# Decode block with its backward pass: V loads queued one iteration later, and seven V tiles of batch 0 kept instead of six

## The chip, the cores and the metric

The kernel runs on one core of a Trainium2 chip. The metric is the device time of one launch in microseconds (us). Five runs of the kernel before gave 923.03 to 930.29 us, with a median of 924.86 us.

## The reference

The computation is one decode step of a transformer block (two sequences, one token each) and its gradients.

```python
h = x + A(layernorm(x))            # attention against a cache, 32 heads, 4096 keys of 128
h2 = h + B(layernorm(h))           # dense layer 640 -> 1728 -> 640 with relu
# A: q = x @ wq; s = q k^T * Dh**-0.5; p = softmax(s); o = p v; o @ wo
out, vjp = jax.vjp(f, A_x, A_k_cache, A_v_cache, A_wq, A_wo, B_w1, B_w2)
grads = vjp(grad_out)              # out, and a gradient for each of the seven inputs
```

For each of the 64 pairs of batch and head, K (4096 x 128, bf16, 1 MB) and V (the same size) are read. Their gradients gK and gV, of the same size again, are written. Everything else is small next to these 256 MB. The gradient of the scores needs V once more: dp = go V^T, where go is the gradient of the head's output, which is known only when the forward pass of the whole batch row and the dense layer are done.

## The kernel before, in words

The work is written out by hand in one order. A plan is a list of pairs (i, j). With i, a step of phase 1 (`p1_iter`) is emitted: scores, softmax and weighted sums of head i. With j, a step of phase 2 (`p2_iter`): the gradients gK and gV of turn j. Steps 0 to 31 are phase 1 of batch 0. Steps 32 to 40 are phase 1 of batch 1 alone, while the dense layer of batch 0 and the go of its first heads are worked out in small background pieces in between. From step 41 every second step has a turn of phase 2 too (the mixed stage, to step 65). After that phase 2 runs alone, with the outer products of the weight gradients beside it.

`p1_iter(i)` is a pipeline over three heads. It transposes K(i) on TensorE in four groups (L416), copies them out of PSUM (L421), and multiplies them by q (L427). It does the softmax of head i-1 and multiplies K(i-1) by it on VectorE (L478). And for head i-2 it multiplies V(i-2) with this product (L471, 32 matmuls, first used right after the first two transpose groups of K(i) and a small matmul L517). K(i-1)'s buffer is given back in the sixth of eight parts of iteration i, V(i-2)'s in the last.

`p2_iter(j)` transposes V again (L437), multiplies it by go (L450), and makes gV and gK by outer products on VectorE (L823), which GpSimd's queue stores.

K, V, the second reading of V (called W) and some weight pieces are loaded by the SP queue, strictly in the order of one list, `queue`. It is built before the work is emitted. For plan step n it gets: perhaps a piece of wq, then K(i), then the W that step n+1 will need, then V(i-1), then perhaps other weights. `pump`, called after each part, takes loads from the head of the list as long as a buffer is free. There are twelve buffers of 1 MB for all these. So the list sets the order, and the giving back of a buffer sets when the next load can be issued.

`KEPT` says of how many last heads of each batch V stays in its buffer from phase 1 to phase 2; for these no W is loaded. `turns` puts them first in phase 2. So before, the buffers that are left for the other loads fall from twelve to six towards the middle. When the first three kept tiles have been used, their buffers become output buffers for gK and gV; nine stay for loads.

`middle_gen` takes the heads of a batch for go in groups: first two kept heads, then the other kept heads, then groups of up to eight. A go takes one reduction on VectorE (L650) per head, and `bg_until` sees to it that a turn's go is there before its turn.

Of the kernel before, what the change touches and what calls it, by code (L numbers as in the profile page):

```python
# [15 lines left out]
def kernel(  # L16
# [101 lines left out]
    def share(**want):  # L118

        wanted.clear()  # L120
        wanted.update(want)
        for tag in homes:
            while free[tag] > 0 and goes_to(tag) != tag:
                to = goes_to(tag)
                homes[to].append(homes[tag].pop(0))
                for d in (free, owned):
                    d[tag] -= 1
                    d[to] += 1

    def more_home(tag, pool):  # L130
        homes[tag].append(len(pools))
        pools.append(pool)
        free[tag] += 1
        owned[tag] += 1
# [256 lines left out]

    pairs = [(b, h) for b in range(B) for h in range(H)]
    NP1 = len(pairs)
    KEPT = (6, 5)
    turns = [(b, h) for b in range(B) for h in (*range(H - KEPT[b], H), *range(H - KEPT[b]))]
    turn_of = {bh: j for j, bh in enumerate(turns)}
    kept = {(b, h) for b in range(B) for h in range(H - KEPT[b], H)}
    u_bank = [None]
# [325 lines left out]
    def middle_gen(b):  # L724
# [66 lines left out]

        first = H - KEPT[b]
        bounds = [(first, first + 2), (first + 2, H)] if b == 0 else [(first, H)]
# [271 lines left out]
    while i <= NP1 + 1 or j <= NP1:  # L1065
        ii = i if i <= NP1 + 1 else None
# [7 lines left out]
    queue = []  # L1074
    W_AT = (10, 15, 20, 24, 31)
    W2_AT = (8, 13, 18)
    for n, (ii, jj) in enumerate(plan):
        if ii is not None:
            if ii % QP == 3 and (ii + 3) // QP < NQ:
                queue.append(("wq", (ii + 3) // QP))  # L1080
            if ii < NP1:
                queue.append(("K", ii))
        ahead = plan[n + 1][1] if n + 1 < len(plan) and ii is not None else jj
        if ahead is not None and ahead < NP1 and turns[ahead] not in kept and ("W", ahead) not in queue:
            queue.append(("W", ahead))
        if ii is not None and 1 <= ii <= NP1:
            queue.append(("V", ii - 1))
        if ii in W_AT:
            queue.append(("w", W_AT.index(ii)))
        if ii in W2_AT:  # L1090
            queue.append(("w2", W2_AT.index(ii)))
# [34 lines left out]
    for n, (i, j) in enumerate(plan):  # L1126
# [4 lines left out]
        if i is None and plan[n - 1][0] is not None:  # L1131
            pkp.release()
            big1 = tc.alloc_tile_pool(name="big1", bufs=1)
            more_home("ld", big1)
            share(ld=KEPT[1] + 4, g=4)
        if all_go and not late[0]:
# [6 lines left out]
        if fin is not None and not bg2 and not bg3:  # L1143
            share(ld=8 + 3 * more, g=6 + 3 * more)
        elif fin is not None and j >= H + KEPT[1] - 1:
            share(ld=5 + 2 * more, g=4 + 2 * more, f=3 + more, q=2 + more)
# [99 lines left out]
```

## Time and profile before

| | before |
|---|---|
| median of 5 runs | 924.86 us |
| the profiled execution | 925.49 us |
| its span | 923.6 us |
| PE, DVE, ACT, POOL busy | 760.3, 662.4, 531.0, 168.4 us |
| moved by DMA | 363.04 MB, mean 393 GB/s |
| Kt, Vt, Wt loads of 1 MB | 64, 64, 53 |
| gK, gV stores of 1 MB | 64, 64 |
| mean granted TensorE clock | 0.784 |

Times in the profile are us from the span's start. The DMA share is the mean busy share of the sixteen DMA engines. A load's landing time is counted from its issue on the SP queue, so it holds the wait behind other transfers too. An engine's idle time costs nothing where another engine or the transfers set the pace.

### The profile page before, as it was taken

The numbers are of one execution on the slowest core, as the hardware profiler recorded it, in microseconds if no ns is written. First come the engines' busy times: TensorE is split into PE (matmuls) and PEld (weight loads), VectorE is DVE, ScalarE is ACT, GpSimd is POOL, SyncE is SP. The second block draws the span as 40 slices with busy tenths as digits, with TensorE's granted clock in tenths as the row PEclk, the third lists the DMA queues.
The fourth block names the chain that finished last, engine by engine and source line by source line (L and its number), as shares of the span: only waits on it lengthen the run. The fifth ranks groups of instructions, "written<-read, shape, count | busy, mean of one in ns | idle before, by whom it ended". The sixth has DMA issues, their size and how long they took to land.

```text
span 923.6 us, 26951 instructions
## 1 busy us (share of the span) xinstructions
PE 760.3 (82%) x11482; PEld 639.8 (69%) x11482; DVE 662.4 (72%) x1237; ACT 531.0 (57%) x1082; POOL 168.4 (18%) x329
## 2 busy tenths in 40 slices
PE   5998998999988898798878826966878887888892
PEld 5887787888877787687767726755757566666661
DVE  4654786876777888678778879868698454558774
ACT  4564564556776777577733625544646555557661
POOL 1222222223200101011011112111122111112211
PEclk9998999999999999899995866556655557556556
DMA  8999999998789999999999999999999999989998
GB/s 345 418 399 411 404 395 411 410 415 321 291 318 363 365 399 422 423 392 422 423 388 396 406 426 379 399 379 408 398 402 388 426 424 425 423 358 355 423 422 352
DMA packets 59480, 363.04 MB, mean 393 GB/s; under 512 B 5696, under 2 KB 15552, under 8 KB 19168
## 3 DMA queue, kind: packets, MB, share of 16 engines
q1 hardware_dynamic: 37920, 212.18, 58.2%
q0 software_dynamic: 18432, 134.23, 35.0%
q10 hardware_dynamic: 3008, 14.91, 4.1%
q8 instruction: 90, 1.47, 0.6%
q14 instruction: 30, 0.25, 0.1%
HBM read 212.16 MB, written 149.13 MB: 391 GB/s over the span
## 4 chain that ended last, share of the span: by engine, by line
PE 39%; DMA 29%; DVE 15%; ACT 10%; issue 5%; POOL 0%; ACTq 0%; POOLq 0%; SPq 0%; DVEq 0%
DMA Kt<-in_A_k_cache_dram 13%; DMA out_dram<-gK 9%; PE t_ps L437 8%; PE t_ps L416 7%; PE m_ps L471 7%; DMA out_dram<-gV 5%; DVE gV L823 4%; DVE gK L823 4%; ACT t_sb L421 4%; PE o_ps L927 3%; DMA wqs<-in_A_wq_dram 3%; PE s_ps L427 3%; ACT t_sb L442 2%; DVE pk L478 2%; PE u_ps L500 2%
## 5 line engine op out<-in xcount | busy, mean ns | idle before, releaser
L421 ACT COPY t_sb<-t_ps 128x1024 bf16<-128x1024 bf16 x223 | 217.4, 1017 | 60.6 <-PE t_ps L416 59.9
L442 ACT COPY t_sb<-t_ps 128x512 f32<-128x512 f32 x256 | 149.4, 587 | 147.4 <-PE t_ps L437 143.8
L437 PE MATMUL t_ps<-ident_f,Wt 128*128 128x128 f32 x848 | 193.5, 375 | 3.2 <-ACT t_sb L421 2.8
L478 DVE TENSOR_TENSOR pk<-Kt,ep 128x2048 bf16<-128x2048 bf16 x128 | 156.4, 1222 | 54.1 <-ACT ep L526 26.2
L416 PE MATMUL t_ps<-ident_bf,Kt 128*128 128x128 bf16 x2048 | 155.2, 226 | 27.3 <-DMA Kt<-in_A_k_cache_dram 21.0
L471 PE MATMUL m_ps<-pk,Vt 128*128 128x129 bf16 x2048 | 172.6, 223 | 1.1 <-ACT OU L584 1.1
L823 DVE TENSOR_TENSOR gK<-rb,gsp 128x2048 bf16<-128x2048 bf16 x128 | 152.3, 1225 | 22.4 <-DMA out_dram<-gK 16.2
L823 DVE TENSOR_TENSOR gV<-rb,pp 128x2048 bf16<-128x2048 bf16 x128 | 152.6, 1218 | 20.9 <-DMA out_dram<-gV 13.9
L437 PEld LDWEIGHTS t_ps<-ident_f,Wt 128*128 128x128 f32 x848 | 134.5, 195 | 27.8 <-issue 18.4
L416 PEld LDWEIGHTS <-Kt 128*128 128x128 bf16 x2048 | 127.3, 101 | 35.0 <-DMA Kt<-in_A_k_cache_dram 22.0
L471 PEld LDWEIGHTS <-Vt 128*128 128x128 bf16 x2048 | 126.7, 99 | 29.4 <-issue 29.4
L450 PEld LDWEIGHTS <-t_sb 128*128 128x128 bf16 x2048 | 95.6, 106 | 39.3 <-ACT t_sb L442 19.1
L450 PE MATMUL dp_ps<-gom,t_sb 128*128 128x2 bf16 x2048 | 95.2, 168 | 9.4 <-ACT t_sb L442 8.3
L488 POOL COPY pk<-ep 128x16 bf16<-128x16 bf16 x80 | 64.0, 803 | 194.9 <-ACT ep L526 165.7
L427 PE MATMUL s_ps<-qc,t_sb 128*128 128x1 bf16 x2048 | 88.1, 164 | 3.7 <-ACT t_sb L421 2.5
L861 POOL DMA_DIRECT2D out_dram<-gK x64 | 34.0, 531 | 282.8 <-DVE gK L823 212.7
L880 POOL DMA_DIRECT2D out_dram<-gV x64 | 34.2, 534 | 265.1 <-DVE gV L823 220.0
L427 PEld LDWEIGHTS <-t_sb 128*128 128x128 bf16 x2048 | 77.2, 96 | 6.7 <-ACT t_sb L421 3.4
L936 ACT CAST ot<-o_ps 128x512 bf16<-128x512 f32 (+4 forms) x134 | 59.4, 479 | 13.9 <-DMA out_dram<-ot 7.8
L583 ACT CAST MT<-m_ps 128x128 bf16<-128x128 f32 x64 | 17.1, 266 | 74.9 <-PE m_ps L471 74.8
L650 DVE CUSTOM_DVE_ANT_0 junk<-wo_t,hbc 128x640 bf16<-128x640 bf16 x64 | 52.4, 818 | 0.2
L850 ACT ACTIVATE rb<-dp_ps,rt 128x256 bf16<-128x256 f32 x64 | 30.4, 475 | 36.1 <-PE dp_ps L845 35.4
(195 smaller groups left out, 785.0 us busy)
## 6 DMA issues: line engine op xcount, KB each, us to landing
Kt<-in_A_k_cache_dram SPq DMA_DIRECT2D x64, 1024.0 KB, 14.0
Vt<-in_A_v_cache_dram SPq DMA_DIRECT2D x64, 1024.0 KB, 14.7
out_dram<-gV POOLq DMA_DIRECT2D x64, 1024.0 KB, 11.4
out_dram<-gK POOLq DMA_DIRECT2D x64, 1024.0 KB, 10.5
Wt<-in_A_v_cache_dram SPq DMA_DIRECT2D x53, 1024.0 KB, 12.8
wo_t<-in_A_wo_dram SPq DMA_DIRECT2D x4, 1280.0 KB, 19.3
wqs<-in_A_wq_dram SPq DMA_DIRECT2D x5, 1024.0 KB, 18.8
wq_t<-in_A_wq_dram SPq DMA_DIRECT2D x5, 960.0 KB
```

Of the source, the lines that this page charges most:

```text
L416: nc.tensor.transpose(t_ps[:, j, :], nat[:, g * GT + j, :], ident_bf[:])
L421: nc.scalar.copy(out=t_sb[:], in_=t_ps[:])
L427: nc.tensor.matmul(dst[:, sc:sc + 1], lhsT=t_sb[:, j, :], rhs=vec, start=True, stop=True)
L437: nc.tensor.transpose(t_ps[:, j, :], natf[:, 2 * cc:2 * cc + 2, :].rearrange("p c k -> p (c k)"), ident_f[:])
L442: nc.scalar.copy(out=t_sb[:], in_=t_ps[:])
L450: nc.tensor.matmul(dst[:, sc:sc + 2], lhsT=v[:, j, :, par], rhs=vecs[:, par, :], start=(par == 0), stop=(par == 1))
L471: nc.tensor.matmul(r["m"][:, 0:129], lhsT=r["V"][:, sc, :], rhs=r["pk"][sc // HALF][:, sc % HALF, 0:129], start=(sc == 0), stop=(sc == NSC ...
L478: nc.vector.tensor_tensor(out=p["pk"][k][:, :, 0:128].rearrange("p s (a two) -> p s a two", two=2), in0=p["K"][:, sl, :].rearrange("p s (a ...
L488: nc.gpsimd.tensor_copy(out=col, in_=e)
L650: nc.vector.tensor_tensor_reduce(out=junk[0:kc, 0:width], in0=in0, in1=in1, scale=1.0, scalar=0.0, op0=ALU.mult, op1=ALU.add, accum_out=acc)
L823: nc.vector.tensor_tensor(out=pairs_view(dst[:, sl, :]), in0=row.rearrange("p (a two) -> p a two", two=2)[:, None, :, :].to_broadcast([128 ...
L936: nc.scalar.copy(out=ot[0:P, k, n0:n0 + nn], in_=o_ps[0:P, 0:nn])
```

## The change

Two edits, both in how the loads are listed. V(i-2), not V(i-1), is put into the list at step i, so each V stands one step later, behind K(i) and behind the W of the next step, and its load is issued in the iteration that comes one later. The list ends with V(63) at step 65. And seven last heads of batch 0, 25 to 31, keep their V; the first seven turns of phase 2 are these heads, and head 0 is turn 7. W is loaded for 52 turns. The middle's groups of go heads become (25, 26), (27 to 31), then 0 to 7, 8 to 15, 16 to 23 and 24.

```diff
-    KEPT = (6, 5)
+    KEPT = (7, 5)
@@ the list of loads, at plan step n with (ii, jj)
         ahead = plan[n + 1][1] if n + 1 < len(plan) and ii is not None else jj
         if ahead is not None and ahead < NP1 and turns[ahead] not in kept and ("W", ahead) not in queue:
             queue.append(("W", ahead))
-        if ii is not None and 1 <= ii <= NP1:
-            queue.append(("V", ii - 1))
+        if ii is not None and ii >= 2:
+            queue.append(("V", ii - 2))
```

## The prediction, made before the result

> **What bounds the kernel now.** I read the page first: how full the sixteen DMA engines are in each of the 40 slices, and how fast they move data.
>
> ```profile
> span 923.6 us, 26951 instructions
> ...
> PE 760.3 (82%) x11482; PEld 639.8 (69%) x11482; DVE 662.4 (72%) x1237; ACT 531.0 (57%) x1082; POOL 168.4 (18%) x329
> ...
> DMA  8999999998789999999999999999999999989998
> GB/s 345 418 399 411 404 395 411 410 415 321 291 318 363 365 399 422 423 392 422 423 388 396 406 426 379 399 379 408 398 402 388 426 424 425 423 358 355 423 422 352
> ```
>
> The DMA engines are full nearly everywhere (363 MB at 393 GB/s), except in slices 10 to 12 and a little after. The busy times by stage (window, then busy us and count of each engine, the granted clock, the DMA share, GB/s) say where exactly:
>
> ```profile
> core 0: us, PE busy (x) PEld busy (x) DVE busy (x) ACT busy (x) POOL busy (x), PEclk, DMA share, GB/s
> 0.00:208.00 208.00, 185.07 (x3585) 162.68 (x3586) 134.72 (x286) 112.75 (x221) 55.81 (x110) 0.97 1.01 401
> 208.00:269.00 61.00, 57.23 (x1131) 50.68 (x1128) 46.08 (x126) 42.02 (x79) 15.86 (x28) 0.97 0.82 313
> 269.00:320.00 51.00, 44.26 (x830) 38.78 (x828) 39.81 (x87) 36.98 (x77) 6.16 (x8) 1.00 0.90 348
> 320.00:466.00 146.00, 126.52 (x2350) 112.72 (x2346) 112.15 (x227) 101.60 (x212) 14.72 (x25) 0.95 1.01 413
> 466.00:923.00 457.00, 347.17 (x3610) 274.98 (x3606) 329.68 (x513) 237.65 (x495) 75.89 (x158) 0.60 0.99 399
> ```
>
> Batch 0's scores (to 208 us), the mixed stage from 320 and the gradients from 466 run at a DMA share of 0.99 to 1.01: transfers set their pace. The middle (208 to 269, iterations 32 to 40, no stores) is different: share 0.82, and PE busy 57.2 of 61.0. Time added there is added to the end, because the transfers can't use it. Now the SP queue's own timeline in the middle (start, duration of the issue, instruction):
>
> ```profile
> 243.27 0.33 SPq L458 DMA_DIRECT2D Kt<-in_A_k_cache_dram  x1
> 243.69 0.38 SPq L458 DMA_DIRECT2D Vt<-in_A_v_cache_dram  x1
> 249.70 0.33 SPq L458 DMA_DIRECT2D Kt<-in_A_k_cache_dram  x1
> 250.12 0.38 SPq L458 DMA_DIRECT2D Vt<-in_A_v_cache_dram  x1
> 255.92 0.33 SPq L458 DMA_DIRECT2D Kt<-in_A_k_cache_dram  x1
> 256.34 0.38 SPq L458 DMA_DIRECT2D Vt<-in_A_v_cache_dram  x1
> ```
>
> One K and one V per iteration, each the moment a buffer comes free, V 0.4 us behind K. The first pair is K38 and V37. V's landing in this stretch (225 to 302 us, the tile view of Vt), and PE's timeline where iterations 38 and 39 begin:
>
> ```profile
> DMA to landing us min/median/max: 6.8/7.6/7.9
> ```
>
> ```profile
> 248.11 1.07 PE L416 MATMUL t_ps<-ident_bf,Kt 128*128 128x128 bf16 x16
> 249.83 0.23 PE L517 MATMUL s_ps<-neg_ident,rmax 128*128 128x128 bf16 x1 [0.66 <-ACT t_sb L421]
> 249.93 0.63 PE L471 MATMUL m_ps<-pk,Vt 128*128 128x129 bf16 x8
> ...
> 256.42 0.63 PE L471 MATMUL m_ps<-pk,Vt 128*128 128x129 bf16 x8
> ```
>
> The reader is to see the distance: K38 is first used at 248.11, V36 at 249.93. V is needed only 1.8 us after K.
>
> **The change part by part.** *One load less.* Head 25's V stays in its buffer, so one of 53 W loads goes: 1.05 MB, at 393 to 415 GB/s 2.5 to 2.7 us of DMA time. What it is worth depends on what is prefetched when the middle ends. Counting the owners of the twelve buffers at the start of iteration i there: before, six kept and K(i), K(i-1), V(i-2), V(i-1), K(i+1), V(i); after, seven kept and K(i), K(i-1), V(i-2), K(i+1), V(i-1). One V less is prefetched, one W less is wanted: what remains to be moved after the middle is the same. The saving is spent as more idle DMA time in the middle, so I cost it at 0 (best case -2.7).
>
> *K one load earlier in the full stretch to 208 us.* An iteration needs K(i), and 1.8 us or less later V(i-2). Before, V(i-2) lay ahead of K(i) in the queue; now it lies behind. The same bytes must land before the first L471, so only the little work between the two uses starts earlier. At iteration 32, where the full stretch ends, K32 is used at 210.0 and V30 at 210.9; K32 would land about 2.6 us earlier, at 207.4, V30 at 210.0 to 210.4. Gain 0.5, at most 2.6.
>
> *V with two buffers in turn, not three.* This is the cost. V(i) now takes the place in the queue, and the buffer release, where before V(i+1) was issued; K's places don't move. PE takes instructions in order, so a late V holds all behind L471: m_part, the next transposes L416, the scores L427, the interleaved gradient matmuls L437 and L450, and so ACT's and DVE's work on them. Issue place of before's next V, plus landing time, less before's first use of V(i):
> - V36: 243.7 + 7.6 = 251.3, used at 249.9: 1.4 late
> - V37: 250.1 + 7.6 = 257.7, used at 256.4: 1.3 late
> - V38: 256.3 + 7.6 = 263.9, used at 263.5: 0.4 late
> - V39: 262.8 + 7.6 = 270.4, used at 269.7: 0.7 late
> - V40 to V44: 0.2 to 2.8 us early.
>
> V(i) is used two iterations on, and its issue moves only with delays up to iteration i, so delay D obeys D(i+2) = max(D(i+1), D(i) + lateness): 1.4, 1.4, 1.8, 2.1. The middle costs 2.1 us.
>
> Here a rule can be set against the row. The Trainium skill ("DMA: Bandwidth & Descriptors", section "Anatomy of one DMA — SWDGE (gpsimd) path") puts a transfer, on GpSimd's path, at 2.0 us plus bytes at 436 GB/s: 4.4 us for one tile, 6.8 with a K just ahead. V36 would be 0.6 late, V37 0.5, V38 and V39 none: 0.6 us. These loads come from SP, and the trace has 5.0 for K and 7.6 for V, so I take the row, 2.1.
>
> With the stores of the mixed stage, landings grow. The V issued at 328.2 took 9.7 us; from 345 on the least is 10.2, the median 15.3. On the same footing: V45, 311.4 + 9.7 against 319.4, 1.7 late; V47, 328.2 + 9.7 against 335.5, 2.4 late; V49, 342.6 + 10.2 against 350.4, 2.4 late; V46 and V48 on time; V50 onward early, because nine load buffers with few kept give the Vs room again (the first W load now comes two iterations later too). Sum 6.5. The skill's section "Queues, rings and completion order" says that a DMA engine takes turns between queues packet by packet. A load beside a store would then have half the rate: 2.0 + 4 x 2.4 = 11.6 us for a V behind a K, where the row has 9.7. By the rule V45 and V47 would be 3.6 and 4.3 late, and the mixed sum 10.3. I take the row again. How much of 6.5 counts? Transfers are full from 320, and PE later waits for K (1.4 at 366.6, 5.7 at 387.3, 3.4 at 439.8), so a delay can run into a wait that exists anyway. But it delays stores and buffer releases too. Bounds 0 and 6.5; nothing in the trace separates them, I take half, 3.2.
>
> *The end of the scores.* W(12) and W(13) now stand ahead of V62 and V63. V63 takes the place of 464.9 instead of 456.8; with about 8 us it lands at 472.9, used at 470.8: 2.1 late, in a full stretch; half, 1.0 (bounds 0 and 2.1).
>
> *Order of the go work.* The second group of batch 0 has five heads, not four, so one reduction of 0.82 us on DVE (L650) moves forward, none is added; it is due at iteration 45. If its slots were gone it would cost at most those 0.8 us. Taken at 0.
>
> Sum: -0.5 + 2.1 + 3.2 + 1.0 = +5.8 us. The profiled execution took 925.5 us (span 923.6 and 1.9 around it), 0.6 above the median of 924.9; on the median 930.7, say 930.5.
>
> **The rivals.** *All of the lateness counts* (and repeats): 2.1 + 6.5 + 2.1 - 0.5 = +10.2, 935; by the take-turns rule +14, 939. For it: PE, in order, stands 1.8 us behind K. Against: transfers are full from 320. *The delay is hidden*: V lands as the page's figure has it, and the mixed stage absorbs the rest: -0.5 + 0.6 to 2, about 925.5. For it: margins in the middle are about 1 us, within what DMA times scatter. *Faster*: PE's waits for K go.
>
> ```profile
> PE t_ps L416 <- DMA Kt<-in_A_k_cache_dram: 21.0, 9, 5.7
> ```
>
> Nine waits, 21.0 us. With K one load (2.5 us) earlier each could lose up to 2.5; taken wait by wait that is 15 us at most. It decides if V isn't what is waited for next, which needs V's use more than 2.5 us behind K's; 1.0 to 1.8 is seen. With half of it, 917.5. Last, *it doesn't do what it says*: W for the next iteration still goes ahead of V for this one, so the order isn't by need in the mixed stage; that is in the sum as V63.
>
> **How the numbers follow.** Chances: the forecast (927 to 936) 0.46, all of it counting (935 to 942) 0.14, hidden (921 to 928.5) 0.26, faster 0.14. The predicted time is the first's, 930.5. Leaving out the top of the second and most of the last gives 919.5 to 939. A measurement of this kernel tells about 0.5%, 4.6 us, from no change: slower means above 929.5. The first case lies above it with 0.37 of its 0.46, the second wholly: 0.51. Same: 0.09 + 0.25 = 0.34. Faster: 0.14 + 0.01 = 0.15.
>
> **What would show it.** After: 52 Wt loads; a wait of L471 for the DMA of Vt, none before, of 1 to 2 us near 250 and 2 us or more between 320 and 355; the waits of L416 for Kt down; a DMA share in 208 to 269 below 0.82. The forecast is wrong if L471 shows no such waits (hidden), or if the stretch from 320 to 466 is shorter than 146 us (faster).

## The result, and the profile after

The changed kernel takes 928.96 us (median of 29 runs), the kernel before 924.89 us (50 runs beside them). The ratio is 1.0045, with a 95% interval of 1.0031 to 1.0058: 4.1 us slower, where 5.6 were forecast (930.5 against 924.9). The lines of the page that answer to those shown of before:

```profile
span 927.9 us, 26947 instructions
...
PE 768.7 (83%) x11482; PEld 644.9 (70%) x11482; DVE 663.5 (72%) x1237; ACT 531.9 (57%) x1082; POOL 174.7 (19%) x329
...
DMA  9999999997779989999999999999999999989998
GB/s 345 417 396 409 407 394 409 412 415 300 288 260 345 348 326 423 423 422 421 423 395 396 409 425 396 405 410 391 401 413 393 426 426 424 420 344 368 421 418 343
```

One load is gone: 361.99 MB instead of 363.04. Yet slices 10 to 15 move less in sum (1,867 instead of 2,057 in the six GB/s figures). The busy times by stage of the changed kernel (columns as before):

```profile
core 0: us, PE busy (x) PEld busy (x) DVE busy (x) ACT busy (x) POOL busy (x), PEclk, DMA share, GB/s
0.00:208.00 208.00, 186.86 (x3594) 163.06 (x3595) 134.96 (x286) 112.79 (x221) 55.73 (x110) 0.97 1.01 400
208.00:269.00 61.00, 56.20 (x1061) 49.68 (x1058) 43.50 (x118) 40.18 (x76) 16.11 (x25) 0.92 0.74 278
269.00:320.00 51.00, 44.71 (x816) 39.03 (x813) 37.80 (x83) 35.72 (x75) 4.97 (x11) 0.97 0.89 337
320.00:466.00 146.00, 126.62 (x2310) 111.98 (x2308) 112.57 (x227) 101.99 (x209) 19.17 (x26) 0.94 0.99 406
466.00:923.00 457.00, 354.35 (x3722) 281.15 (x3718) 334.70 (x527) 241.27 (x504) 78.70 (x159) 0.60 1.00 404
```

In the middle (208 to 269) the DMA share fell from 0.82 to 0.74, and 278 GB/s instead of 313 over 61 us are 2.1 MB less moved, two loads. One is the V that is no longer prefetched; the other I put down to the delay. Two columns moved that the prediction had not looked at. PE is hardly less busy in the middle (56.2 instead of 57.2) although it executed 70 matmuls fewer, and its granted clock fell from 0.97 to 0.92. PE's waits for transfers, from the view of waits:

```profile
PE m_ps L471 <- DMA Vt<-in_A_v_cache_dram: 21.0, 16, 2.9
```

Before, it was nine waits of L416 for Kt, also 21.0 us in sum. The tile that is waited for has changed; the sum has hardly changed (three waits for Kt, 3.4 us, are left beside these). Now the middle itself: the SP queue's timeline, and then PE's, of the changed kernel.

```profile
242.46 0.33 SPq L458 DMA_DIRECT2D Kt<-in_A_k_cache_dram  x1
242.88 0.38 SPq L458 DMA_DIRECT2D Vt<-in_A_v_cache_dram  x1
248.71 0.33 SPq L458 DMA_DIRECT2D Kt<-in_A_k_cache_dram  x1
249.13 0.67 SPq L458 DMA_DIRECT2D Vt<-in_A_v_cache_dram  x1
258.18 0.33 SPq L458 DMA_DIRECT2D Kt<-in_A_k_cache_dram  x1
```

```profile
247.29 1.07 PE L416 MATMUL t_ps<-ident_bf,Kt 128*128 128x128 bf16 x16
248.84 0.23 PE L517 MATMUL s_ps<-neg_ident,rmax 128*128 128x128 bf16 x1 [0.49 <-DVE rmax L573]
251.30 1.05 PE L471 MATMUL m_ps<-pk,Vt 128*128 128x129 bf16 x8 [2.23 <-DMA Vt<-in_A_v_cache_dram]
...
252.55 1.04 PE L416 MATMUL t_ps<-ident_bf,Kt 128*128 128x128 bf16 x8
...
255.23 1.04 PE L500 MATMUL u_ps<-pk,hot 128*32 128x512 bf16 x8
...
258.44 1.05 PE L416 MATMUL t_ps<-ident_bf,Kt 128*128 128x128 bf16 x16
```

The V at 242.88 is V36: the same place in the queue, 0.4 us behind K38, held V37 before. PE finishes the first transposes of K38, and then waits 2.23 us for V36. What follows is not only later but slower: the eight V matmuls take 1.05 us instead of 0.63, L500 1.04 instead of 0.62. From V36's first use to K39's it is 7.1 us (251.3 to 258.4); before, it was 4.8 (249.9 to 254.7). K39's first use before:

```profile
254.70 1.07 PE L416 MATMUL t_ps<-ident_bf,Kt 128*128 128x128 bf16 x16
```

How far iteration i is behind the kernel before, from the first L416 of each (us; one profiled execution of each kernel, all but the first are experiments):

| | K32 | K38 | K39 | K44 | K45 | K47 | K48 | K52 | K56 | K60 | K61 | K63 | span |
|---|---|---|---|---|---|---|---|---|---|---|---|---|---|
| changed | -1.5 | -0.8 | +3.7 | +2.6 | +4.8 | +3.8 | +8.3 | +9.9 | +2.7 | +9.1 | +5.5 | +5.1 | +4.2 |
| seven kept alone | +0.2 | +3.6 | +4.4 | +5.0 | +6.8 | +10.3 | +11.6 | +14.2 | +5.5 | +11.9 | +9.0 | +10.0 | +8.3 |
| V later alone | -2.3 | -1.9 | -2.2 | -2.0 | -2.1 | -2.0 | -2.0 | -2.0 | -4.7 | -1.3 | -4.9 | -1.3 | -4.3 |
| eight kept, V later | -2.2 | +13.0 | +17.3 | +41.3 | +42.5 | +49.6 | +55.3 | +62.0 | +51.9 | +58.9 | +55.3 | +57.2 | +56.7 |
| changed, waits filled | -2.5 | +1.2 | +3.6 | +3.8 | +4.6 | +4.0 | +7.0 | +8.3 | +0.3 | +5.7 | +2.4 | +3.7 | +4.7 |
| one W less | 0.0 | +0.2 | 0.0 | 0.0 | +0.2 | -0.6 | -0.5 | +0.3 | -4.8 | -0.1 | -1.1 | -0.5 | -2.9 |

In the changed kernel there are two steps of 4.5 us: at V36 (K38 to K39), and at V45 (K47 to K48, a wait of 2.49 us at 325.9, again with slow matmuls behind it). Between them stands a third, of 2.2 us (K44 to K45), which is not a wait for a load. It is the go work of the second group, heads 27 to 31. Before, VectorE was through with the reductions of that group, then four heads, at 285.6 us:

```profile
285.58 0.17 DVE L673 CAST goc<-go 128x4 bf16<-128x4 f32 x1
```

In the changed kernel the fifth reduction (L650) comes behind a gV product that waits for an output buffer, and PE waits for the group:

```profile
299.93 1.23 DVE L823 TENSOR_TENSOR gV<-rb,pp 128x2048 bf16<-128x2048 bf16 x1 [3.27 <-DMA out_dram<-gK]
301.07 0.82 DVE L650 CUSTOM_DVE_ANT_0 junk<-wo_t,hbc 128x640 bf16<-128x640 bf16 x1
...
301.94 0.17 DVE L673 CAST goc<-go 128x5 bf16<-128x5 f32 x1
```

```profile
302.16 0.19 PE L337 MATMUL pr_ps<-goc,sel 128*128 128x5 bf16 x2 [2.63 <-DVE goc L673]
```

The kernel before waits in this iteration too, 2.11 us at 300.8 for a copy of ScalarE, but at full clock from there on; in the changed kernel the clock is at half for 3.4 us behind the wait. All four profiles with seven kept have this wait of L337 (2.2 to 2.8 us), those with five, six or eight have none.

In the full stretch behind, 7 us of 9.9 are gone at K56, but they come back: it is 9.1 at K60. Most of that dip belongs to the profile of before, which waited 5.7 us for K55. The run with one W less issues the same loads in the same order as the kernel before until past K63; it is level with it at K52 and K60, and 4.8 us ahead at K56. So one column of this table can be off by about 5 us. What does go is 3.6 us at K61, where the kernel before waited 3.4 us for K61 and the changed one did not.

### The profile page after: what moved, and what is told of

Read it like the earlier page. It is cut to its first block, busy times and chain, and to the rows that moved or that the text cites. A ratio compares the mean times of both kernels' runs of the same rounds, so it can differ in the third digit from the quotient of the medians.

```text
span 927.9 us, 26947 instructions
## 1 busy us (share of the span) xinstructions
PE 768.7 (83%) x11482; PEld 644.9 (70%) x11482; DVE 663.5 (72%) x1237; ACT 531.9 (57%) x1082; POOL 174.7 (19%) x329
## 2 busy tenths in 40 slices
DMA packets 59336, 361.99 MB, mean 390 GB/s; under 512 B 5680, under 2 KB 15536, under 8 KB 19152
## 4 chain that ended last, share of the span: by engine, by line
PE 33%; DMA 32%; DVE 11%; ACT 7%; issue 4%; POOL 0%; SPq 0%; POOLq 0%; ACTq 0%; DVEq 0%
DMA Vt<-in_A_v_cache_dram 15%; PE t_ps L437 8%; DMA out_dram<-gV 7%; DMA out_dram<-gK 7%; PE m_ps L471 6%; PE t_ps L416 5%; DVE gV L823 4%; DVE gK L823 3%; DMA wqs<-in_A_wq_dram 3%; PE o_ps L927 2%; ACT t_sb L442 2%; PE dp_ps L450 2%; ACT t_sb L421 2%; PE u_ps L500 2%; PE s_ps L427 2%
## 5 line engine op out<-in xcount | busy, mean ns | idle before, releaser
L437 PE MATMUL t_ps<-ident_f,Wt 128*128 128x128 f32 x832 | 191.5, 378 | 2.6 <-ACT t_sb L421 2.6
L471 PE MATMUL m_ps<-pk,Vt 128*128 128x129 bf16 x2048 | 175.4, 226 | 21.4 <-DMA Vt<-in_A_v_cache_dram 21.0
L823 DVE TENSOR_TENSOR gV<-rb,pp 128x2048 bf16<-128x2048 bf16 x128 | 152.6, 1218 | 21.7 <-DMA out_dram<-gV 8.5
L471 PEld LDWEIGHTS <-Vt 128*128 128x128 bf16 x2048 | 127.9, 100 | 55.3 <-issue 31.3
L823 DVE TENSOR_TENSOR gK<-rb,gsp 128x2048 bf16<-128x2048 bf16 x128 | 152.4, 1225 | 17.9 <-DMA out_dram<-gK 14.0
L416 PE MATMUL t_ps<-ident_bf,Kt 128*128 128x128 bf16 x2048 | 157.6, 228 | 8.6 <-DMA Kt<-in_A_k_cache_dram 3.4
L416 PEld LDWEIGHTS <-Kt 128*128 128x128 bf16 x2048 | 129.4, 102 | 15.7 <-issue 8.3
L450 PEld LDWEIGHTS <-t_sb 128*128 128x128 bf16 x2048 | 95.9, 106 | 38.0 <-ACT t_sb L442 19.1
L427 PEld LDWEIGHTS <-t_sb 128*128 128x128 bf16 x2048 | 78.9, 98 | 3.5 <-DVE t_sb L419 1.3
L650 DVE CUSTOM_DVE_ANT_0 junk<-wo_t,hbc 128x640 bf16<-128x640 bf16 x64 | 52.3, 818 | 0.2
## 6 DMA issues: line engine op xcount, KB each, us to landing
Wt<-in_A_v_cache_dram SPq DMA_DIRECT2D x52, 1024.0 KB, 11.9
```

Source lines behind the costliest of these rows:

```text
L416: nc.tensor.transpose(t_ps[:, j, :], nat[:, g * GT + j, :], ident_bf[:])
L427: nc.tensor.matmul(dst[:, sc:sc + 1], lhsT=t_sb[:, j, :], rhs=vec, start=True, stop=True)
L437: nc.tensor.transpose(t_ps[:, j, :], natf[:, 2 * cc:2 * cc + 2, :].rearrange("p c k -> p (c k)"), ident_f[:])
L450: nc.tensor.matmul(dst[:, sc:sc + 2], lhsT=v[:, j, :, par], rhs=vecs[:, par, :], start=(par == 0), stop=(par == 1))
L471: nc.tensor.matmul(r["m"][:, 0:129], lhsT=r["V"][:, sc, :], rhs=r["pk"][sc // HALF][:, sc % HALF, 0:129], start=(sc == 0), stop=(sc == NSC ...
L650: nc.vector.tensor_tensor_reduce(out=junk[0:kc, 0:width], in0=in0, in1=in1, scale=1.0, scalar=0.0, op0=ALU.mult, op1=ALU.add, accum_out=acc)
```

## The experiments

Ratios are to runs of the kernel before on the same chip, with 95% intervals.

**The two edits apart.** Theory A: the seventh kept tile takes a buffer from the middle, and whichever tile then has two buffers in turn and not three comes late. Theory B: V's place in the queue makes it late.

```diff
# seven kept alone (from the kernel before)
-    KEPT = (6, 5)
+    KEPT = (7, 5)
# V later alone (from the changed kernel)
-    KEPT = (7, 5)
+    KEPT = (6, 5)
```

> Seven V tiles of batch 0 kept, V listed where the kernel before lists it (V(i-1) at step i). Theory A (rotation: the seventh kept tile takes a buffer from the loads of the middle, and whichever tile loses its third buffer comes late): in the middle five buffers hold K(i), K(i-1), V(i-2), V(i-1), K(i+1), so now K(i+2) takes the later place behind V(i). K38 would land at 243.7 + 7.6 = 251.3 against a use at 248.1: 3 us late, K40 and K41 1 to 2 us; waits of L416 for Kt in the middle, none of L471 for Vt, and a time no better than that of the change: 929 to 935. Theory B (the queue's order alone makes V late): no cost here, and one load less: 922 to 925.

> Six V tiles kept, V listed one step later as in the change. Theory A: the middle has six buffers for K(i), K(i-1), V(i-2), K(i+1), V(i-1), K(i+2); V(i) is issued no later than in the change but a K is far ahead of it, so it lands in about 5 us instead of 7.6: no wait of L471 in 230 to 300 us, the time 923 to 926, equal to before. Theory B (order): V still stands behind K and W, so the waits of L471 stay and the time is 928 to 930.

Seven kept alone: 933.14 us, 1.0104 (1.0079 to 1.0129). V later alone: 923.06 us, 0.9986 (0.9962 to 1.0010). From the views of waits in 208 to 320 us, first seven kept alone, then V later alone:

```profile
PE t_ps L416 <- DMA Kt<-in_A_k_cache_dram: 6.6, 4, 4.0
```

```profile
PE m_ps L471 <- DMA Vt<-in_A_v_cache_dram: 1.4, 1, 1.4
```

Theory A holds, B is out. With seven kept in the old order K is late (K38 by 4.0 us); with V later and six kept PE waits for no load in this window after the one wait at 210. Of the two edits the kept tile costs about 9 us, and V's later place wins about half of that back. The table says the same: seven kept alone has lost 14.2 us at K52. Not all of the 9 us is the buffer: the wait for the go work, 2.2 us in this run, comes with the seventh head as well, and what it is worth in the end was not tested apart.

**One buffer less still.**

```diff
-    KEPT = (7, 5)
+    KEPT = (8, 5)
```

> The change with eight V tiles of batch 0 kept (one W load less again, one buffer less again in the middle). Theory A: four buffers hold K(i), K(i-1), V(i-2), K(i+1); V(i-1) can be issued only when K(i-1) is given back in iteration i and is used about 4 us later, so it comes 1 to 3 us late in every iteration from about 34 to 48, and the time rises by 15 to 40 us, to 945 to 970. Theory B (order): V's place in the list is that of the change, so the time stays within 926 to 932.

980.09 us, 1.0620 (1.0553 to 1.0687): 56 us, above what A said. Waits in 208 to 320 us and the busy times there:

```profile
PE m_ps L471 <- DMA Vt<-in_A_v_cache_dram: 29.1, 9, 4.6
```

```profile
208.00:269.00 61.00, 46.49 (x800) 41.02 (x798) 32.05 (x84) 31.35 (x58) 14.35 (x19) 0.81 0.58 218
269.00:320.00 51.00, 35.67 (x540) 31.10 (x538) 25.07 (x65) 23.56 (x45) 4.64 (x12) 0.79 0.49 187
```

V is late in every iteration, as A said, but by up to 4.6 us where A had 1 to 3. That is one part of why the size was off. The other is the granted clock of 0.8 there: the trace's record of it shows half clock for 3.4 to 6.8 us behind nearly every one of these waits. Of the 38 us that the delay grew from K33 to K43 (320 us), 28 are the waits themselves.

**Is the half clock part of the price?** In the two iterations with the long waits matmuls without use fill the time in which PE would wait.

```diff
+        if i in (38, 47):
+            for k in range(32):
+                nc.tensor.matmul(p["bank"][:, 320:448], lhsT=c["K"][:, k % 16, :], rhs=c["K"][:, k % 16 + 1, :],
+                                 start=True, stop=True)
         if r is not None:
             m_part(0)
             m_part(1)
```

> The changed kernel with 32 matmuls without use (128x128, on K that is there) put ahead of the V matmuls L471 of iterations 38 and 47 alone, where the changed kernel's PE waited 2.2 and 2.5 us for V36 and V45 and ran at half clock for 6.8 us behind each wait. V still lands when it lands. Theory A1 (the half clock is part of the price): the granted clock stays at 1.00 from 251 to 258, K39's first use goes from 3.7 us behind the kernel before to 1 to 2 us behind, and the whole to 926 to 927.5. Theory A2 (the time behind the wait is hidden later by full transfers): K39 comes earlier all the same, but the whole stays at 928 to 930.

929.46 us, 1.0043 (1.0027 to 1.0059). The window of 251 to 258 us, in the kernel before, the changed kernel and the filled one, and the filled one's PE timeline:

```profile
251.00:258.00 7.00, 6.33 (x132) 5.55 (x130) 6.86 (x19) 5.33 (x12) 1.68 (x4) 1.00 0.85 315
```

```profile
251.00:258.00 7.00, 6.70 (x78) 5.41 (x79) 3.87 (x8) 2.65 (x5) 2.36 (x2) 0.51 0.63 265
```

```profile
251.00:258.00 7.00, 6.23 (x114) 5.43 (x115) 5.00 (x14) 3.60 (x7) 2.06 (x3) 1.00 0.82 308
```

```profile
252.00 1.95 PE L522 MATMUL s_ps<-Kt 128*128 128x128 bf16 x32 [0.64 <-DVE nb L519]
253.79 0.63 PE L471 MATMUL m_ps<-pk,Vt 128*128 128x129 bf16 x8
...
256.17 0.62 PE L500 MATMUL u_ps<-pk,hot 128*32 128x512 bf16 x8
```

Locally the clock's part is shown. With PE busy through the wait the clock stays at 1.00, L471 takes 0.63 us, and the steps in the table shrink from 4.5 to 2.4 us (K38 to K39) and from 4.5 to 3.0 (K47 to K48). But the whole did not gain: A2 was right, or the gain is below the 1 to 2 us that these intervals leave open. This profile also has a half-clock stretch of its own, 209.5 to 216.3, behind a wait of 1.4 us for V30, which cost 3.8 us between K32 and K33; the changed kernel's wait there was 0.6 us, without it. So a microsecond won at one place can be lost at another from one execution to the next. The wait for the go work, 2.4 us here, is not touched by the filling.

**V ahead of W.**

```diff
+        if ii is not None and ii >= 2:
+            queue.append(("V", ii - 2))
         ahead = plan[n + 1][1] if n + 1 < len(plan) and ii is not None else jj
         if ahead is not None and ahead < NP1 and turns[ahead] not in kept and ("W", ahead) not in queue:
             queue.append(("W", ahead))
-        if ii is not None and ii >= 2:
-            queue.append(("V", ii - 2))
```

> The change with one exchange: at each step V(i-2) is listed ahead of the W of the next step (order of need throughout). If the W ahead of V costs in the mixed stage: the wait of 2.1 us of L471 at 478 goes and those at 393 to 463 shrink, time 1 to 2 us below the change, about 927. If the mixed stage and its end are set by transfers anyway, the waits move to W or K and the time stays at 928 to 930. The waits at 251 and 326 stay under both, because no W is loaded before 350.

> Six kept, V one step later, and V ahead of W. Six kept with V later showed no V wait in the middle and 0.9986 of before; its waits of L471 from 360 to 470 come with a W ahead of V. If those cost: 1 to 2 us less than with W first, 921 to 922. If transfers set that stretch: 922.5 to 924, as with W first.

With seven kept 929.55 us, 1.0065 (1.0040 to 1.0090); with six kept 924.59 us, 0.9986 (0.9959 to 1.0014), the same ratio as with W first. With seven kept the wait for V63 at 478 is gone, the waits at 250 and 324 are there (2.4 us each), and five waits of 0.5 to 2.3 us remain in 390 to 462. In the full stretch V's place beside W is worth nothing that these intervals can show.

**What a load is worth.** One W load left out where transfers are full, and one W load added by keeping five, with V later and with V as before.

```diff
# one W less (from the kernel before), in p2_iter and in the list
+        if j == 19:
+            S2[20] = {"W": c["W"]}
+        else:
             give(c["W"], "g" if j < H and owned["g"] < 3 else None)
-        if ... turns[ahead] not in kept and ("W", ahead) not in queue:
+        if ... turns[ahead] not in kept and ahead != 20 and ("W", ahead) not in queue:
# five kept
+    KEPT = (5, 5)
```

> The kernel before, but turn 20 takes the W tile of turn 19 (its dp and gK are then of the wrong head): one load of 1.05 MB left out, all buffers and the order of V as before, and no effect on the middle. If a load in the full stretch is worth its transfer time: 2.5 to 2.7 us faster than before, about 922. If the stretch is set by something else: equal to before, 924 to 925.

> Five kept, V one step later: one buffer more in the middle than with six, one W load more. By the count of buffers the extra load is fetched in the idle transfer time of the middle and costs nothing: 922 to 925, the same as with six kept and V later (923.1). If a load costs its transfer time wherever it is: 2.6 us more, 925.5 to 926.5.

> Five kept, V listed as before. By the count of buffers the middle has a seventh one for one more prefetched tile, and the one more W load is paid there: equal to before, 924 to 926. If a load costs its transfer time anywhere: 2.6 us more, about 927.5.

One W less: 923.16 us, 0.9972 (0.9956 to 0.9989): 2.6 us (1.0 to 4.1), which agrees with the transfer time. Five kept: with V later 923.58 us, 0.9977 (0.9959 to 0.9996), with V as before 925.33 us, 0.9999 (0.9977 to 1.0021). So a load costs about 2.6 us in the full stretch, but the load that a sixth kept tile saves costs nothing when it is put back: an added 2.6 us (1.0028) lies outside both intervals. The freed buffer prefetches more in the middle, as the row of five kept with V as before shows (share 0.86 and 333 GB/s, against 0.82 and 313 in the kernel before):

```profile
208.00:269.00 61.00, 56.03 (x1135) 49.45 (x1131) 46.49 (x128) 42.44 (x80) 15.58 (x28) 1.00 0.86 333
```

A kept tile's saving is paid with the buffer that it sits in.

**Six kept in batch 1.** V's later place gives a buffer back at the end of the scores. Can one more tile of batch 1 be kept for it?

```diff
-    KEPT = (7, 5)
+    KEPT = (6, 6)          # and (5, 6)
-            share(ld=KEPT[1] + 4, g=4)
+            share(ld=KEPT[1] + 3, g=4)     # left as it was in the third
```

> V one step later, six kept in batch 0 as before, and six instead of five in batch 1, with nine load buffers and four output buffers when phase 2 runs alone, as before (so three instead of four for W beside the kept). One W load is saved in a stretch where a load is worth its time (2.6 us by the run with one W less), and V's later place gives the buffer back at the end of the scores: 920 to 922. If three W buffers are too few for phase 2: slower than before, 927 or more.

> The same with five kept in batch 0 (0.9977 of before with five in batch 1). If the two add: 920 to 921.5. If three W buffers are too few: 927 or more.

> As with six and six, but with the share of the code as it stands, ten load buffers and three output buffers while phase 2 runs alone. If the stores wait for output buffers: 2 to 6 us slower than with nine and four; if W buffers were the short ones: faster than it.

No gain: 927.09 us, 0.9999 (0.9984 to 1.0013), and 925.71 us, 0.9995 (0.9978 to 1.0013), so neither the forecast gain nor a clear loss. What became of the 2.6 us of the saved load was not settled; transfers are still full (share 0.99 from 466 us on before, 1.00 from 466 to 900 with six and six). Taking an output buffer instead costs 22 us where 2 to 6 were expected, 948.75 us, 1.0235 (1.0202 to 1.0268). From 466 to 900 us VectorE's waits for stores (L823) are 41 us there and 28 with nine and four, and the transfers are no longer full:

```profile
466.00:900.00 434.00, 326.62 (x3265) 260.19 (x3264) 295.82 (x475) 213.58 (x443) 66.91 (x141) 0.56 0.95 376
```

No version beats the kernel before by more than 0.3%: five kept with V later has the lowest ratio of those that leave no work out, 0.2% faster with an interval that barely leaves 1 out, and V later alone is not to be told from before.

## Why the prediction was right, and where its sizes were off

The direction and the first cause were right: with one buffer less V comes late behind K, first at V36, and PE waits for it. 930.5 was forecast, 928.96 measured, within the range and the likeliest case's own. That the size came so near is in part luck: the clock behind the waits was left out and the go work put at 0, and against that the waits of the mixed stage were summed to 6.5 us where 4.0 were measured, and 5.7 of 9.9 us of delay went again where the forecast let 4.4 of 10.2 go. Step by step:

- *One load less is worth 0.* Right, and shown from both sides: 2.6 us for a load in the full stretch, nothing for a kept tile given up, within 2 us.
- *K one load earlier, -0.5.* K32 came 1.5 us earlier, the iterations behind it 1.1. Nearer the forecast than the -2.6 of its bound; V30's wait at 210.2 (0.6 us) took part of the lead.
- *V with two buffers in turn, middle: 2.1.* V36 was first used at 251.3, 1.4 us later than before, as forecast; the wait is 2.2 us because PE came 0.8 us earlier. V37 was on time, as the recurrence said. V38 and V39 cost no wait, where 0.4 and 0.3 more stood. So the waiting was well sized. What was missing is the clock: half speed for 6.8 us behind the wait, 2.3 us more, and K39 is 3.7 us behind. The page of before had half-clock stretches too (its row of the granted clock has its dips, at 75 and 386 us behind waits for K), and the prediction didn't put a price on them.
- *Order of the go work: 0, at most 0.8.* The term that was put too low. The one reduction that moved forward got behind a gV product that waited 3.27 us for an output buffer, PE waited 2.63 us for it at 302.2, and the delay grew by 2.2 us from K44 to K45. The bound of 0.8 counted the reduction's own time and not what stands ahead of it on VectorE.
- *The mixed stage: V45, V47 and V49 late by 1.7, 2.4 and 2.4.* Measured 2.5, 0.8 and 0.7: V45 again with half clock behind it, 4.5 us between K47 and K48; that this delay left the next ones less to wait for is likely, not shown. The delay reached 9.9 us at K52.
- *Half is taken in by full transfers.* About right as a share, for what can be seen: of 9.9 us at K52 and 9.1 at K60, 5.1 were left at K63 and 4.2 in the span. The mechanism is seen at one place of this pair of profiles, at K61: the delay ran into a wait for K that existed anyway. Where the other 2 us went is not shown.
- *The end of the scores: V63 2.1 late, half of it counts.* 2.14 us late, at 478.3. With V ahead of W this wait is gone and the time no better: it counted for nothing that can be seen.
- *The rules set against the rows.* For the landing the rows were the better ones: V took 6.9 to 8.2 us in the middle, median 7.1, between the 6.8 of the rule and 7.6 of the row. By the rule V36 would have been 0.6 later than before; it was 1.4. By the rule of turns V47 would have been 4.3 late; it waited 0.8, with a delay already there.
- *Faster, because waits for K go.* They went (21.0 us before, 3.4 after), and 21.0 us of waits for V took their place, as the rival's counter-argument had it: V's use stands 1.0 to 1.8 us behind K's.

## What to carry to other kernels

A tile that is kept saves a load and holds a buffer. Where transfers later are full but a middle stretch is not, the buffer is what fills the idle transfers of that stretch, and keeping one tile more can cost more than its load. Count, for each stretch that is not bound by transfers, how many buffers each stream has in turn, and compare the time from a buffer's release to its next use with the time from issue to landing: here 7.6 us against 6.2 decided (V36: a buffer free at 243.7 in the kernel before, first used at 249.9). And look at what else the number of kept tiles moves: here one short reduction came due earlier, and cost more than its own length because of what stood ahead of it in its engine's order.

## What was not expected

A short wait on PE can cost more than itself where it stands. In the changed kernel all eight waits of L416 and L471 for a load of 1.1 us or more, up to 2.9 us, were followed by a granted clock of 0.5 for 3.4 or 6.8 us, and none of the shorter ones; the same groups took 1.05 and 1.04 us instead of 0.63 and 0.62. In the kernel before, those of 3.2 us and more were, and three of 1.1 to 1.5 us were not, nor was the wait of 2.11 us for ScalarE at 300.8, so there is no sharp limit in these traces. The Trainium skill ("TensorE: Matmul & The Clock Gate", Part 1 on the clock gate) describes half and full speed as the only two, set by activity windows of about 3.4 us, and puts the fall to half at a whole idle window; the lengths here, 3.4 and 6.8 us, agree with the windows, but waits of 1.2 to 2.9 us, under a window, were enough. That matmuls without use keep the clock up is shown; that this was worth nothing over the whole kernel is, within 1 to 2 us, too.

Nor is a busy PE enough. In the changed kernel PE was busy for all of 3.4 us and had half clock for the next 3.4:

```profile
230.60:234.00 3.40, 3.40 (x107) 3.37 (x105) 1.61 (x4) 0.83 (x3) 1.41 (x2) 0.99 0.96 337
234.00:237.40 3.40, 3.40 (x35) 3.40 (x34) 0.97 (x6) 2.23 (x4) 0.09 (x1) 0.50 0.96 393
```

The kernel before has the same at 235.4 us. In both, 70 of the matmuls just before are those of the dense layer (L749), with one column each; whether that is the reason was not tested.
